# Two chunks' products with the old states interleaved in the first segment, one chunk with its heads in changed rows

## The chip, the cores and the metric

The kernel runs on one core of a Trainium2 chip. The time is that of the device in microseconds (us), from the start of the program on the core to its end; several executions are taken and the median counts. The engines of a core work side by side, each on its own list of instructions in order: PE (TensorE, matrix products), DVE (VectorE), ACT (ScalarE) and POOL (GpSimd). SP (SyncE) only issues loads and stores (DMA) here. An instruction that waits holds up everything behind it on its own engine, and nothing else.

## What is computed

A recurrent attention (RetNet) and behind it a gated feed-forward block, in 32-bit floats:

```python
# q, k, v: (B, H, S, D) = (4, 8, 768, 64)
gamma = 1.0 - 2.0 ** (-5.0 - np.arange(H))
state = zeros(B, H, D, D)
for t in range(S):
    state = gamma[None, :, None, None] * state + einsum('bhd,bhe->bhde', k[:, :, t], v[:, :, t])
    y[:, :, t] = einsum('bhd,bhde->bhe', q[:, :, t], state) / sqrt(D)
x = y.transpose(0, 2, 1, 3).reshape(3072, 512)
g, val = x @ w_gate, x @ w_val          # 512 x 1536 each
out = (g / (1 + exp(-g)) * val) @ w_out  # 1536 x 512
```

The weights arrive as 64-bit floats, and the kernel converts them itself.

## The kernel before

**Tiling.** The sequence of each batch is cut into 6 chunks of 128 positions, and a segment is three chunks of two batches. Four segments make the work. Within a chunk, attention is done with matrix products: scores of q and k under a mask of decays, times v, plus q (scaled by the decay since the chunk's start) times the old state that the chunks before left behind; then the state is decayed and grown by k and v. The feed-forward part of the segment follows: the up part with 12 slices of 128 columns of w_gate and w_val (units f = 0 to 11), the down part with 12 row blocks of w_out. Operands of those products are split into three terms of a shorter format (the tiles `oitem`, `gitem`, `xa`: near_a, near_b, near_c for weights, far_a, far_b, far_c for x), on ACT, DVE and POOL.

**The first segment** (its chunks are numbered n = 0 to 5: n even is the first batch, n odd the second) has to do everything at once: load q, k and v, do the attention, load the weights' 64-bit words, convert them, store the converted ones for the later segments, and run the products. A written plan, `PLAN`, sets the order in which all instructions are issued, and so the order on each engine. Its letters (table at line 577) are:

- `l n:w` loads chunk n's k (w = 0), q (1), v (2), k by rows (3); `U`, `V` load words of weights (unit 0's w_gate with `U0`, its w_val with `V0`; `U12` is the first of w_out); `A` loads tables; `Z` stores a converted unit.
- `s` scores (PE) and masks (DVE); `r`, `t` (state) and `g` (decay of the state, ACT); `m` scores times v (PE) and far_a; `x` far_b and far_c; `o` the product of q with the old state (PE, `mix_old`, line 726); `q`/`Q` scale q with the table qdec on POOL/DVE; `k`/`K`/`E` scale k on POOL/DVE/ACT.
- `a`, `b`, `c` on ACT and `S`, `C` on DVE are the steps that convert a piece of a weight; `T` makes the differences of a unit's parts that later segments need (`sums_t`, line 563), on DVE; `n` the near split of unit f; `p`, `v`, `u`, `y` its products for one chunk, the gate and their product, which empties the PSUM bank (line 948).

**The product with the old state** has 64 rows (the head's dimension) in, 64 out and 128 positions. Two heads lie one above the other: the upper half of the partitions holds head 2n, the lower half head 2n + 1, for q, k and the state. `mix_old` takes the eight heads in turn, so that two of the four quadrants of the PE array are used in turn, upper rows to upper columns and lower rows to lower columns:

```python
for k, (n, i, to) in enumerate(y_parts(c)[1]):
    r = ds(D * i, D)
    nc.tensor.matmul(to, prev[r, n], qd[r, n], start=k < 2, ...)
```

**Loads.** All loads go through SP's queue in the plan's order and use eight completion semaphores in turn, so that an issue waits for the load eight before it. `w_load` (line 1128) brings the blocks of w_out in the down part: in the last segment in two pieces for f < 3, else in one.

Of the kernel before, what the change touches and what calls it, by code (L numbers as in the profile page):

```python
# [25 lines left out]
L = 3  # L26
TH = L * P
NSEG = B * NCK // (2 * L)
# [21 lines left out]

PLAN = """
    A0 I0 l0:0 l1:0 A2 A1 U0:0 s0 a0:1 r1 l0:2 s1 b0:1 A4 A3 l2:1 l2:0 r0 m0 K0 S0:1 c0:1 l1:2 x0:1
    t0 s2 E1 l3:0 l3:1 m1 l2:3 C0:1 g2 V0:0 a0:0 Q2 n0:0 b0:0 l2:2 x1:2 s3 x1:1 n0:1 l4:1 l4:0 l3:2
    t1 S0:0 k2 x0:2 q3 c0:0 C0:0 o2 U1:1 m2 o3 n0:3 s4 m3 a1:1 n0:4 x2:1 l5:1 l3:3 b1:1 x2:2 x3:1
    S1:1 t2 n0:2 p0:0 q4 a1:0 x3:2 c1:1 n0:5 k3 C1:1 g3 b1:0 n1:0 v0:0 l5:0 U2:3 s5 S1:0 t3 c1:0
    C1:0 l5:2 p0:1 n1:1 u0:0 u0:1 T0:0 q5 v0:1 a2 l4:2 b2 y0:1 o5 y0:0 o4 n1:3 S2 n1:2 m5 T0:1 n1:4
    c2 m4 n1:5 x5:2 p1:0 l5:3 x5:1 p1:1 u1:0 C2 v1:0 U3:1 T0:2 x4:2 T1:0 U12:0 a3 v1:1 y1:0 x4:1
    T1:1 L b3 p0:2 a12 c12 n2:0 S3 u1:1 T1:2 b12 u0:2 U4:3 c3 Z0 n2:1 v0:2 Z1 n2:3 S12 y1:1 a4 n2:2
    p1:2 v1:2 C3 u1:2 n2:4 G2:0 y0:2 C12 G2:1 n3:0 U13:1 y1:2 n3:1 n2:5 b4 T2:0 n3:2 S4 U5:2 n3:3
    c13 T2:1 W2:0 Z12 W2:1 h0 c4 i2:1 n3:4 i2:0 G3:0 n3:5 T3:0 C4 T2:2 T3:1 U6:3 j2:0 a5 G3:1 T3:2  # L60
    j2:1 Z2 n4:0 U7:0 W3:0 i3:0 n4:1 b5 n4:2 n4:3 S5 n4:4 W3:1 i3:1 n4:5 c5 G4:0 C5 n5:0 a6 b6 a13
    l4:3 T4:0 j3:0 G4:1 n5:1 j3:1 Z3 T4:1 n5:3 i4:0 n5:2 T4:2 S6 W4:0 b13 c6 i4:1 n5:4 a7 S13 C6
# [246 lines left out]
T0, UP0 = 30.0, 8.35  # L309
# [61 lines left out]
def tile_retnet_swiglu(  # L371
# [13 lines left out]
    nc = tc.nc  # L385
# [30 lines left out]
    loads = place("loads", 3 * UNIT + 256)  # L416
# [6 lines left out]
    warm = place("warm", P + 32)  # L423
# [36 lines left out]
    chunks = {}  # L460

    def load_chunk(n, w, queue=nc.sync):
        c = cs[n]
        t = early[4 * n + w]
        chunks.setdefault(c, {})[w] = t
        queue.dma_start(out=t, in_=(k_t, q_t, v_n, k_n)[w][c])  # L466

    def seg_chunks(s):
        p, pos = divmod(s * L, NCK)
# [5 lines left out]
    T3, B22, B12, T1, B21, B11, T2, T4 = 0, 1, 2, 2, 3, 4, 5, 6  # L475
# [87 lines left out]
    def sums_t(piece, parts=range(3)):  # L563
        kind, a = piece
        w = wt[a]
        flat = w.rearrange("p a b -> p (a b)")
        n = KH * P
        pair = flat[:, : 4 * n].rearrange("p (a b) -> p a b", b=2 * n)[:, :, :n]
        for o, x, y in [((pair, w[:, ds(B22, 2)], w[:, B12 : B11 + 1 : 2])),
                          ((w[:, T2], w[:, B22], w[:, T1])),  # L570
                          ((w[:, T4], w[:, B21], w[:, T2]))][parts[0] : parts[-1] + 1]:
            both(o, x, y, sub)


    pieces = [("up", f) for f in range(NF)] + [("down", a) for a in range(NF // 2)]

    parts = {
        "s": lambda n: scores(cs[n]), "o": lambda n: mix_old(cs[n]),
        "m": lambda n: mix(cs[n]), "x": lambda n, p: split_x(cs[n], p[0]),
        "g": lambda n: decay(cs[n]), "t": lambda n: state(cs[n]),  # L580
        "E": lambda n: scale_k_act(cs[n]),
        "r": lambda n: rows_of(n), "I": lambda n: unit_of(), "B": lambda n: small_tables(),
        "R": lambda n: decay_rows(), "D": lambda n: spread_rows(), "F": lambda n: keep_rows(),
        "k": lambda n: scale_k(cs[n]), "q": lambda n: scale_q(cs[n]),
# [36 lines left out]
    def pairs(t):  # L621
        return t.rearrange("p (n t) -> p n t", n=NP)

    def state_of(c, old=0):
        return states[:, (c + old) % 2, c // NCK % 2]

    def scores(c):
        kt, qt = (pairs(chunks[c][w]) for w in range(2))
        sp = [bank("y" if cs.index(c) == 1 else "s") for i in range(2)]
        for n in range(NP):  # L630
            for i in range(2):
                r = ds(D * i, D)
                nc.tensor.matmul(sp[i][:, ts(n, P)], kt[r, n], qt[r, n],  # L633
                                 start=(n == 0), stop=True, skip_group_check=True)
        a = []
        for i in range(2):
            j = turn["a"] = turn.get("a", -1) + 1
            t = pairs(tmp[:, ts(j % 4, 512)] if j < 10 else loads[:, ts(j - 2, 512)])
            nc.vector.tensor_tensor(t, pairs(sp[i]), mask[:, i], op=ALU.mult)
            a.append(t)  # L640
        att[c] = a


    def scale_q(c, engine=nc.gpsimd):
        if c % NCK:
            qt = pairs(chunks[c][1])
            chunks[c][1] = loads[:, ts(cs.index(c) + 2, 512)]
            engine.tensor_tensor(pairs(chunks[c][1]), qt, qdec, op=ALU.mult)

    def scale_k(c, engine=nc.gpsimd):  # L650
        if c % NCK < NCK - 1:
# [14 lines left out]
    def unit_of():  # L666
        nc.vector.tensor_scalar(unit, mask[:, 0, 0], 0.124, None, op0=ALU.is_ge)
# [21 lines left out]
    def rows_of(n):  # L689
# [4 lines left out]
            nc.tensor.transpose(t[:, ts(m, P)], kt[:, m], unit)  # L694
        chunks[c][3], turned[c] = early[4 * n + 3], t

    def decay(c):

        if 0 < c % NCK < NCK - 1:
            for n in range(NP):  # L700
                nc.scalar.activation(state_of(c)[:, n], state_of(c, 1)[:, n], AF.Copy,
                                     scale=gdec[:, ds(n, 1)])

    def state(c):
        ci = c % NCK
        if ci == NCK - 1:
            return
        vn, kd = chunks[c][2], chunks[c][3]
        new = state_of(c)
        st = banks[6][:, : NP * D]  # L710
        st = st.rearrange("p (n e) -> p n e", n=NP)
        for n in range(NP):
            for i in range(2):
                h = ts(2 * n + i, D)
                nc.tensor.matmul(st[ds(D * i, D), n], kd[:, h], vn[:, h],  # L715
                                 start=(n == 0), stop=True, skip_group_check=True)
        if ci == 0:
            nc.scalar.copy(new, st)
        else:
            nc.vector.tensor_tensor(new, new, st, op=ALU.add)  # L720

    def y_parts(c):
        y = pairs(banks[(0, 1, 2, 3, 7, 6)[first_chunks.index(c)]])
        return y, [(n, i, y[ds(D * i, D), n]) for n in range(NP) for i in range(2)]

    def mix_old(c):
        qd, prev = pairs(chunks[c][1]), state_of(c, 1)
        for k, (n, i, to) in enumerate(y_parts(c)[1]):
            r = ds(D * i, D)
            nc.tensor.matmul(to, prev[r, n], qd[r, n], start=k < 2, stop=False,  # L730
                             skip_group_check=True)

    def x_of(c):
        i, j = c // NCK % 2, c % L
# [2 lines left out]
    def split_x(c, part):  # L737
        (far_b, far_c)[part - 1](x_of(c), y_parts(c)[0])
# [15 lines left out]
    lmask = local[:, : 2 * NP * HC].rearrange("p (i n) -> p i n", i=2)  # L754
    lk, lg = local[:, ds(2 * NP * HC, H)], local[:, ds(2 * NP * HC + H, NP)]
    spare = tab[:, : 2 * 512]
    half = [ds(0, D), ds(D, D)]
    given = {}
    R0 = 6

# [367 lines left out]
    def w_load(s, t, f, first):  # L1128
        def load():
            wo[f] = item("o", DM)  # L1130
            o = wo[f].bitcast(U32)
            if first:
                nc.sync.dma_start(out=o[:, 2], in_=w_dn[f].bitcast(U32))
            else:
                for i in (slice(2), slice(2, 3)) if s == NSEG - 1 and f < 3 else (slice(None),):
                    nc.sync.dma_start(out=o[:, i], in_=w_dn3[f][:, i])

        def o():
            return [wo[f][:, i] for i in range(3)]
# [117 lines left out]
    cs = seg_chunks(0)  # L1257
# [21 lines left out]
    t = down_stage(0, end)  # L1279
    for s in range(1, NSEG):  # L1280
# [8 lines left out]
        t = down_stage(s, t)  # L1289
# [50 lines left out]
```

## Time and profile before

| what | value |
|---|---|
| median of three runs | 642.5 us (642.07 to 642.75) |
| profiled execution | 642.54 us |
| its span, first to last instruction | 640.5 us |
| granted PE clock | 1.00 throughout |
| busy: PE, DVE, ACT, POOL | 632.9, 484.1, 394.3, 261.1 us |
| loads and stores | 139.6 MB, 218 GB/s on average |
| PE matmuls of the old states' product (line 730) | 64 passes, 269 ns each, 16.3 to 32.3 us |
| DVE's scaling of q (line 648) | 1, 1269 ns |
| POOL's scaling of q (line 648) | 3, 1271 to 1728 ns |
| DVE's differences of unit 0 | 0.69, 0.42 and 0.42 us, at 30.8, 33.4 and 36.6 |

A 32-bit product appears as two passes of PE in the trace, so 8 products are 16 passes. Passes overlap in the array: the 269 ns are one pass from end to end, while 16 of them start within 1.02 us. A busy share says how long an engine worked; whether it holds up the others is read from who waited for whom. The span has about 18 us at its start in which the first data arrive, and 622 us behind it.

### The profile page before, as it was taken

How to read it: one execution, taken by the hardware profiler on the slowest of the kernel's cores; microseconds unless marked ns; L12 is line 12 of the kernel's file. 1: busy time of each engine (PE TensorE's matmuls, PEld its weight loads, DVE VectorE, ACT ScalarE, POOL GpSimd, SP SyncE). 2: the span in 40 equal slices, each digit the busy share in tenths (PEclk: the TensorE clock that was granted, in tenths of full speed). 3: DMA queues.
4: the chain of work that ended last, by engine and by line, in shares of the span. 5: the costliest groups of instructions: out<-in, count | busy, mean ns of one | idle time of the engine just before them, and what ended most of it. 6: DMA issues, size and time to landing. Idle time of an engine off the chain costs nothing.

```text
span 640.5 us, 14132 instructions
## 1 busy us (share of the span) xinstructions
PE 632.9 (99%) x5587; PEld 580.4 (91%) x5587; DVE 484.1 (76%) x715; ACT 394.3 (62%) x868; POOL 261.1 (41%) x172
## 2 busy tenths in 40 slices
PE   7999999999999999999999999999999999999997
PEld 6899999987779999997778999998777999999886
DVE  4998787899898887665797869575789866768361
ACT  4787797777865565566766555564785555654221
POOL 1534445544425866630003665550101666663000
PEclk9999999999999999999999999999999999999999
DMA  9899998798787445258765640457776444304564
GB/s 320 291 332 326 376 329 269 268 326 305 266 285 278 168 148 173 75 179 260 247 239 214 211 152 15 175 196 246 226 258 248 154 164 173 116 1 151 194 214 148
DMA packets 50626, 139.60 MB, mean 218 GB/s; under 512 B 5120, under 2 KB 18176, under 8 KB 50560
## 3 DMA queue, kind: packets, MB, share of 16 engines
q1 hardware_dynamic: 49984, 137.92, 62.6%
q8 instruction: 44, 0.72, 0.5%
q10 hardware_dynamic: 576, 0.79, 0.3%
q14 instruction: 22, 0.18, 0.1%
HBM read 108.80 MB, written 29.88 MB: 217 GB/s over the span
## 4 chain that ended last, share of the span: by engine, by line
PE 97%; DMA 3%; SPq 0%; DVE 0%; ACT 0%; issue 0%
PE bank L1088 41%; PE bank L1157 32%; PE bank L919 13%; PE bank L789 6%; PE bank L937 3%; DMA hT<-in_v_n_dram 2%; PE bank L744 1%; DMA hT<-in_q_t_dram 1%; PE bank L730 0%; PE bank L715 0%; PE bank L633 0%; DVE chunk_x L1178 0%; SPq L513 0%; ACT chunk_x L1180 0%; SPq L466 0%
## 5 line engine op out<-in xcount | busy, mean ns | idle before, releaser
L1157 PE MATMUL bank<-oitem,gitem 128*128 128x512 f32 x867 | 208.2, 394 | 0.0
L1157 PEld LDWEIGHTS bank<-oitem,gitem 128*128 128x128 f32 x867 | 159.6, 188 | 34.5 <-DVE tmp L812 0.4
L997 POOL TENSOR_TENSOR gitem<-gitem 128x768 fp32r<-128x768 f32 x71 | 138.7, 1963 | 117.9 <-DVE gitem L994 99.0
L1088 PE MATMUL bank<-xa,gitem 128*128 128x384 f32 x864 | 160.5, 334 | 0.0
L1088 PEld LDWEIGHTS bank<-xa,gitem 128*128 128x128 f32 x864 | 150.8, 188 | 0.2
L997 POOL TENSOR_TENSOR oitem<-oitem 128x256 fp32r<-128x256 f32 (+1 forms) x60 | 64.1, 1074 | 56.8 <-DVE oitem L994 48.3
L1088 PE MATMUL bank<-xb,gitem 128*128 128x384 f32 x432 | 84.5, 334 | 0.0
L919 PE MATMUL bank<-xa,oitem 128*128 128x384 f32 x480 | 84.3, 335 | 0.0
L919 PEld LDWEIGHTS bank<-xa,oitem 128*128 128x128 f32 x480 | 83.0, 188 | 0.4 <-ACT tmp L444 0.2
L994 DVE SCALAR_TENSOR_TENSOR gitem<-gitem,loads 128x768 fp32r<-128x768 f32 x72 | 75.1, 1057 | 9.1 <-ACT gitem L991 7.5
L1088 PEld LDWEIGHTS bank<-xb,gitem 128*128 128x128 f32 x432 | 75.9, 188 | 0.4
L991 ACT ACTIVATE gitem<-loads 128x768 fp32r<-128x768 f32 x72 | 59.6, 843 | 26.0 <-PE bank L1088 16.8
L994 DVE SCALAR_TENSOR_TENSOR gitem<-gitem,hT 128x768 fp32r<-128x768 f32 x48 | 46.1, 965 | 24.4 <-ACT gitem L991 24.4
L991 ACT ACTIVATE gitem<-hT 128x768 fp32r<-128x768 f32 x48 | 40.2, 842 | 31.4 <-PE bank L1157 29.4
L1022 ACT COPY chunk_x<-bank 64x128 f32<-64x128 f32 x144 | 36.6, 260 | 32.6 <-PE bank L789 21.3
L401 DVE SCALAR_TENSOR_TENSOR gitem<-gitem 128x768 fp32r<-128x768 f32 x49 | 49.7, 1022 | 1.3 <-DVE gitem L994 0.5
L816 POOL TENSOR_TENSOR loads<-loads,tab 128x512 f32<-128x512 f32 x9 | 13.4, 1493 | 82.1 <-PE bank L789 44.6
L1088 PE MATMUL bank<-xb,oitem 128*128 128x384 f32 x216 | 43.4, 335 | 0.0
L1088 PEld LDWEIGHTS bank<-xb,oitem 128*128 128x128 f32 x216 | 37.9, 188 | 0.3
L994 DVE SCALAR_TENSOR_TENSOR oitem<-oitem,loads 128x256 fp32r<-128x256 f32 (+1 forms) x42 | 34.5, 824 | 2.1 <-ACT oitem L991 2.1
L1105 DVE TENSOR_TENSOR hT<-bank,tmp 128x384 f32<-128x384 f32 x36 | 20.0, 555 | 20.7 <-PE bank L1088 20.4
L1103 ACT COPY tmp<-bank 128x384 f32<-128x384 f32 x36 | 17.2, 478 | 28.3 <-PE bank L1088 19.3
(118 smaller groups left out, 789.8 us busy)
## 6 DMA issues: line engine op xcount, KB each, us to landing
loads<-wup SPq DMA_DIRECT2D x36, 896.0 KB, 4.7
oitem<-wdnt SPq DMA_DIRECT2D x33, 768.0 KB, 4.4
wdnt<-oitem SPq DMA_DIRECT2D x12, 768.0 KB, 5.5
wup<-first SPq DMA_DIRECT2D x9, 896.0 KB, 6.7
rawp<-in_w_gate_dram SPq DMA_DIRECT2D x12, 512.0 KB, 6.8
rawp<-in_w_val_dram SPq DMA_DIRECT2D x12, 512.0 KB, 6.2
rawp<-in_w_out_dram SPq DMA_DIRECT2D x12, 512.0 KB, 5.7
out_dram<-chunk_x SPq DMA_DIRECT2D x21, 256.0 KB, 2.1
```

What stands on the lines that cost most here:

```text
L401: stt(o, x, 1.0, y, op0=mul, op1=op)
L789: nc.tensor.matmul(o, a, b, start=start, stop=True, skip_group_check=True)
L919: nc.tensor.matmul(o, w[:, a, ts(b, P)], X0[:, a, i, NC - 1 - b], start=a == b == 0, stop=a == 2 and b == NC - 1, skip_group_check=True)
L937: nc.tensor.matmul(o, w[:, a, ts(b, P)], X0[:, a, :, NC - 1 - b, ts(j, P)], start=a == b == 0, stop=a == 2 and b == NC - 1, skip_group_che ...
L991: act(o[0], x, AF.Copy, scale=CUT / FAR)
L994: stt(o[1], f32(o[0]), -FAR, x, op0=mul, op1=add)
L997: op(o[2], f32(o[0]), f32(o[1]), op=add)
L1022: copy(cx[half[i], ds(2 * h, 2), c, half[z]], y.rearrange("p (b t) -> p b t", b=2))
L1088: nc.tensor.matmul(o, w[:, a, k], x[:, a, KH - 1 - k], start=start and a == k == 0, stop=a == 2 and k == KH - 1, skip_group_check=True)
L1103: steps = (lambda: copy(p1, x), lambda: tt(c11, z, p1, op=add), lambda: act(gate, c11, AF.Silu, scale=ONE), lambda: copy(u2, x), lambda: c ...
L1105: lambda: copy(p5, wb), lambda: tt(h1, x, p5, op=add),
L1157: nc.tensor.matmul(banks[tok][:, cols], hs[f][:, a, ds(i * TH + u * P, P)], wo[f][:, a, cols], start=f == a == 0, stop=f == NF - 1 and a = ...
```

## The change

`mix_old` now takes two chunks, n and n + 1, and issues their products in turn, head by head. For the second of the two, the heads lie with the halves exchanged ("turned over"): the lower half holds head 2n, the upper one head 2n + 1. Its products go from lower rows to upper columns and from upper rows to lower columns, so that four products in a row lie in four different quadrants. The two chunks write different PSUM banks. To have it so, for the second batch's chunks 3 and 5:

- their k and q are loaded in two halves each, with the halves exchanged (four loads become eight); the scores come out exchanged too and are swapped back by name;
- the state that chunk 1 and chunk 3 leave is written with its halves exchanged (an index of the product), and the decays take a turned copy of their table: two small copies on ACT. Chunk 5's decay turns the state back: eight instructions of 64 partitions where four of 128 were;
- q is scaled with a turned copy of qdec: two copies of 64x512 on DVE.

The product of chunk 3 moves ahead of m2, together with chunk 2's; in the plan q2 becomes POOL's (it was DVE's `Q2`) and stands ahead of q3 and k2. On ACT, the copy of chunk 1's state moves ahead of `a0:0`, `n0:0` and `b0:0`. `sums_t` of unit 0 runs on POOL instead of DVE. In the last segment, `w_load` brings w_out in two pieces for f < 7.

```diff
--- before.py
+++ after.py
@@ -50,16 +50,16 @@
-    t0 s2 E1 l3:0 l3:1 m1 l2:3 C0:1 g2 V0:0 a0:0 Q2 n0:0 b0:0 l2:2 x1:2 s3 x1:1 n0:1 l4:1 l4:0 l3:2
-    t1 S0:0 k2 x0:2 q3 c0:0 C0:0 o2 U1:1 m2 o3 n0:3 s4 m3 a1:1 n0:4 x2:1 l5:1 l3:3 b1:1 x2:2 x3:1
-    S1:1 t2 n0:2 p0:0 q4 a1:0 x3:2 c1:1 n0:5 k3 C1:1 g3 b1:0 n1:0 v0:0 l5:0 U2:3 s5 S1:0 t3 c1:0
-    C1:0 l5:2 p0:1 n1:1 u0:0 u0:1 T0:0 q5 v0:1 a2 l4:2 b2 y0:1 o5 y0:0 o4 n1:3 S2 n1:2 m5 T0:1 n1:4
...
+    e0 e1 t0 s2 q2 E1 l3:0 l3:1 m1 e2 l2:3 C0:1 g2 V0:0 l2:2 x1:2 s3 q3 t1 a0:0 n0:0 b0:0 x1:1 n0:1
+    l4:1 l4:0 l3:2 S0:0 k2 x0:2 c0:0 C0:0 U1:1 o2 m2 s4 n0:3 m3 a1:1 n0:4 x2:1 l5:1 l3:3 b1:1 x2:2
+    x3:1 S1:1 t2 n0:2 p0:0 q4 a1:0 x3:2 c1:1 n0:5 k3 C1:1 g3 b1:0 n1:0 v0:0 l5:0 U2:3 s5 S1:0 t3
+    c1:0 C1:0 l5:2 p0:1 n1:1 u0:0 u0:1 q5 T0:0 v0:1 a2 l4:2 b2 y0:1 y0:0 o4 n1:3 S2 n1:2 m5 T0:1
+    n1:4 c2 m4 n1:5 x5:2 p1:0 l5:3 x5:1 p1:1 u1:0 C2 v1:0 U3:1 T0:2 x4:2 T1:0 U12:0 a3 v1:1 y1:0
...
@@ -463,7 +463,17 @@
         c = cs[n]
         t = early[4 * n + w]
         chunks.setdefault(c, {})[w] = t
-        queue.dma_start(out=t, in_=(k_t, q_t, v_n, k_n)[w][c])
+        src = (k_t, q_t, v_n, k_n)[w][c]
+        if w < 2 and turned_over(c):
+            for m in range(2):
+                queue.dma_start(out=t[half[m]], in_=src[half[1 - m]])
+            return
+        queue.dma_start(out=t, in_=src)
+
+    half = [ds(0, D), ds(D, D)]
+
+    def turned_over(c):
+        return c // NCK % 2 == 1 and c % NCK > 0
 
     def seg_chunks(s):
         p, pos = divmod(s * L, NCK)
@@ -569,16 +579,16 @@
         for o, x, y in [((pair, w[:, ds(B22, 2)], w[:, B12 : B11 + 1 : 2])),
                           ((w[:, T2], w[:, B22], w[:, T1])),
                           ((w[:, T4], w[:, B21], w[:, T2]))][parts[0] : parts[-1] + 1]:
-            both(o, x, y, sub)
+            (pool if a < 1 else both)(o, x, y, op=sub)
 
 
     pieces = [("up", f) for f in range(NF)] + [("down", a) for a in range(NF // 2)]
 
     parts = {
-        "s": lambda n: scores(cs[n]), "o": lambda n: mix_old(cs[n]),
+        "s": lambda n: scores(cs[n]), "o": lambda n: mix_old(cs[n], cs[n + 1]),
         "m": lambda n: mix(cs[n]), "x": lambda n, p: split_x(cs[n], p[0]),
         "g": lambda n: decay(cs[n]), "t": lambda n: state(cs[n]),
-        "E": lambda n: scale_k_act(cs[n]),
+        "E": lambda n: scale_k_act(cs[n]), "e": lambda n: turn_tables(n),
         "r": lambda n: rows_of(n), "I": lambda n: unit_of(), "B": lambda n: small_tables(),
         "R": lambda n: decay_rows(), "D": lambda n: spread_rows(), "F": lambda n: keep_rows(),
         "k": lambda n: scale_k(cs[n]), "q": lambda n: scale_q(cs[n]),
@@ -629,10 +639,12 @@
         sp = [bank("y" if cs.index(c) == 1 else "s") for i in range(2)]
         for n in range(NP):
             for i in range(2):
-                r = ds(D * i, D)
+                r = half[i]
                 nc.tensor.matmul(sp[i][:, ts(n, P)], kt[r, n], qt[r, n],
                                  start=(n == 0), stop=True, skip_group_check=True)
         a = []
+        if turned_over(c):
+            sp = sp[::-1]
         for i in range(2):
             j = turn["a"] = turn.get("a", -1) + 1
             t = pairs(tmp[:, ts(j % 4, 512)] if j < 10 else loads[:, ts(j - 2, 512)])
@@ -645,7 +657,18 @@
         if c % NCK:
             qt = pairs(chunks[c][1])
             chunks[c][1] = loads[:, ts(cs.index(c) + 2, 512)]
-            engine.tensor_tensor(pairs(chunks[c][1]), qt, qdec, op=ALU.mult)
+            engine.tensor_tensor(pairs(chunks[c][1]), qt, qturn if turned_over(c) else qdec,
+                                 op=ALU.mult)
+
+    qturn = pairs(loads[:, :512])
+    gturn = warm[:, ds(P + 8, NP)]
+
+    def turn_tables(m):
+        if m < 2:
+            nc.vector.tensor_scalar(qturn[half[m]], qdec[half[1 - m]], 1.0, None, op0=mul)
+            return
+        for m in range(2):
+            act(gturn[half[m]], gdec[half[1 - m]], AF.Copy)
 
     def scale_k(c, engine=nc.gpsimd):
         if c % NCK < NCK - 1:
@@ -694,12 +717,22 @@
             nc.tensor.transpose(t[:, ts(m, P)], kt[:, m], unit)
         chunks[c][3], turned[c] = early[4 * n + 3], t
 
+    def other(c):
+        return c // NCK % 2 == 1 and c % NCK < L - 1
+
     def decay(c):
 
         if 0 < c % NCK < NCK - 1:
+            new, was = state_of(c), state_of(c, 1)
             for n in range(NP):
-                nc.scalar.activation(state_of(c)[:, n], state_of(c, 1)[:, n], AF.Copy,
-                                     scale=gdec[:, ds(n, 1)])
+                if not turned_over(c):
+                    act(new[:, n], was[:, n], AF.Copy, scale=gdec[:, ds(n, 1)])
+                elif other(c):
+                    act(new[:, n], was[:, n], AF.Copy, scale=gturn[:, ds(n, 1)])
+                else:
+                    for m in range(2):
+                        act(new[half[m], n], was[half[1 - m], n], AF.Copy,
+                            scale=gturn[half[1 - m], ds(n, 1)])
 
     def state(c):
         ci = c % NCK
@@ -712,7 +745,7 @@
         for n in range(NP):
             for i in range(2):
                 h = ts(2 * n + i, D)
-                nc.tensor.matmul(st[ds(D * i, D), n], kd[:, h], vn[:, h],
+                nc.tensor.matmul(st[half[i ^ other(c)], n], kd[:, h], vn[:, h],
                                  start=(n == 0), stop=True, skip_group_check=True)
         if ci == 0:
             nc.scalar.copy(new, st)
@@ -723,12 +756,13 @@
         y = pairs(banks[(0, 1, 2, 3, 7, 6)[first_chunks.index(c)]])
         return y, [(n, i, y[ds(D * i, D), n]) for n in range(NP) for i in range(2)]
 
-    def mix_old(c):
-        qd, prev = pairs(chunks[c][1]), state_of(c, 1)
-        for k, (n, i, to) in enumerate(y_parts(c)[1]):
-            r = ds(D * i, D)
-            nc.tensor.matmul(to, prev[r, n], qd[r, n], start=k < 2, stop=False,
-                             skip_group_check=True)
+    def mix_old(c, d):
+        parts = [(pairs(chunks[e][1]), state_of(e, 1), y_parts(e)[1]) for e in (c, d)]
+        for k in range(2 * NP):
+            for x, (qd, prev, to) in enumerate(parts):
+                n, i, o = to[k]
+                nc.tensor.matmul(o, prev[half[i ^ x], n], qd[half[i ^ x], n], start=k < 2,
+                                 stop=False, skip_group_check=True)
 
     def x_of(c):
         i, j = c // NCK % 2, c % L
@@ -754,7 +788,6 @@
     lmask = local[:, : 2 * NP * HC].rearrange("p (i n) -> p i n", i=2)
     lk, lg = local[:, ds(2 * NP * HC, H)], local[:, ds(2 * NP * HC + H, NP)]
     spare = tab[:, : 2 * 512]
-    half = [ds(0, D), ds(D, D)]
     given = {}
     R0 = 6
 
@@ -1132,7 +1165,7 @@
             if first:
                 nc.sync.dma_start(out=o[:, 2], in_=w_dn[f].bitcast(U32))
             else:
-                for i in (slice(2), slice(2, 3)) if s == NSEG - 1 and f < 3 else (slice(None),):
+                for i in (slice(2), slice(2, 3)) if s == NSEG - 1 and f < 7 else (slice(None),):
                     nc.sync.dma_start(out=o[:, i], in_=w_dn3[f][:, i])
 
         def o():
```

More of the change, by code (lines that the diff above doesn't have):

```diff
@@ L52 @@
     A0 I0 l0:0 l1:0 A2 A1 U0:0 s0 a0:1 r1 l0:2 s1 b0:1 A4 A3 l2:1 l2:0 r0 m0 K0 S0:1 c0:1 l1:2 x0:1
-    t0 s2 E1 l3:0 l3:1 m1 l2:3 C0:1 g2 V0:0 a0:0 Q2 n0:0 b0:0 l2:2 x1:2 s3 x1:1 n0:1 l4:1 l4:0 l3:2
-    t1 S0:0 k2 x0:2 q3 c0:0 C0:0 o2 U1:1 m2 o3 n0:3 s4 m3 a1:1 n0:4 x2:1 l5:1 l3:3 b1:1 x2:2 x3:1
-    S1:1 t2 n0:2 p0:0 q4 a1:0 x3:2 c1:1 n0:5 k3 C1:1 g3 b1:0 n1:0 v0:0 l5:0 U2:3 s5 S1:0 t3 c1:0
-    C1:0 l5:2 p0:1 n1:1 u0:0 u0:1 T0:0 q5 v0:1 a2 l4:2 b2 y0:1 o5 y0:0 o4 n1:3 S2 n1:2 m5 T0:1 n1:4
[L57 to L62, printed above, removed]
+    e0 e1 t0 s2 q2 E1 l3:0 l3:1 m1 e2 l2:3 C0:1 g2 V0:0 l2:2 x1:2 s3 q3 t1 a0:0 n0:0 b0:0 x1:1 n0:1
[3 more added lines that the diff above has]
+    n1:4 c2 m4 n1:5 x5:2 p1:0 l5:3 x5:1 p1:1 u1:0 C2 v1:0 U3:1 T0:2 x4:2 T1:0 U12:0 a3 v1:1 y1:0
+    x4:1 T1:1 L b3 p0:2 a12 c12 n2:0 S3 u1:1 T1:2 b12 u0:2 U4:3 c3 Z0 n2:1 v0:2 Z1 n2:3 S12 y1:1 a4
+    n2:2 p1:2 v1:2 C3 u1:2 n2:4 G2:0 y0:2 C12 G2:1 n3:0 U13:1 y1:2 n3:1 n2:5 b4 T2:0 n3:2 S4 U5:2
+    n3:3 c13 T2:1 W2:0 Z12 W2:1 h0 c4 i2:1 n3:4 i2:0 G3:0 n3:5 T3:0 C4 T2:2 T3:1 U6:3 j2:0 a5 G3:1
+    T3:2 j2:1 Z2 n4:0 U7:0 W3:0 i3:0 n4:1 b5 n4:2 n4:3 S5 n4:4 W3:1 i3:1 n4:5 c5 G4:0 C5 n5:0 a6 b6
+    a13 l4:3 T4:0 j3:0 G4:1 n5:1 j3:1 Z3 T4:1 n5:3 i4:0 n5:2 T4:2 S6 W4:0 b13 c6 i4:1 n5:4 a7 S13 C6
     W4:1 n6:0 T5:0 U8:2 Z4 b7 U14:3 n5:5 n6:1 G5:0 j4:1 S7 C13 j4:0 G5:1 n6:2 a8 n6:3 P2 n6:4 i5:1
```

## The prediction

> **What bounds the kernel now.** First the list of who waited for whom on PE: engine and line, the releaser, total us, times, longest.
>
> ```profile
> PE bank L633 <- DMA hT<-in_k_t_dram: 1.4, 2, 0.9
> PE bank L744 <- DMA hT<-in_v_n_dram: 1.2, 2, 0.6
> PE bank L1253 <- DVE warm L1268: 1.1, 1, 1.1
> PE bank L633 <- DVE tmp L639: 0.4, 1, 0.4
> ```
>
> That is all PE waited for in 640.5 us, and the table by stages shows where: 4.1 us of idle before 18 us, none from 18 to 196.
>
> ```profile
> 0.00:18.00 18.00, 13.91 (x170) 11.98 (x170) 9.94 (x17) 9.31 (x24) 2.93 (x6) 1.00 0.94 327
> 18.00:32.00 14.00, 14.00 (x188) 13.01 (x190) 13.41 (x24) 10.07 (x20) 7.04 (x6) 1.00 0.85 278
> ```
>
> (Stretch, its length, busy us of PE, weight loads, DVE, ACT, GpSimd, clock, DMA share, GB/s.) So time is won by less PE work after 18 us or by filling a wait before it, as long as nothing that feeds PE becomes late. The PE timeline (start, us, ... what ended the idle time) has the work concerned:
>
> ```profile
> 15.56 0.69 PE L715 MATMUL bank<-hT 128*64 128x64 f32 x16
> 16.25 1.09 PE L730 MATMUL bank<-loads,states 64*64 64x128 f32 x16
> 17.97 1.09 PE L744 MATMUL bank<-tmp,hT 128*64 128x128 f32 x16 [0.63 <-DMA hT<-in_v_n_dram]
> 18.99 1.09 PE L730 MATMUL bank<-loads,states 64*64 64x128 f32 x16
> 20.02 1.16 PE L633 MATMUL bank<-hT 64*128 64x128 f32 x16
> 30.43 1.96 PE L730 MATMUL bank<-loads,states 64*64 64x128 f32 x32
> ```
>
> L730 is the old states' product: chunk 2 (16.25) and chunk 3 (18.99) with m2 between them, waiting for its v until 17.97; chunks 4 and 5 together at 30.43. Last, the timelines of DVE, ACT and SP give the chain that could make PE wait:
>
> ```profile
> 14.93 1.27 DVE L648 TENSOR_TENSOR loads<-hT,tab 128x512 f32<-128x512 f32 x1
> 19.12 0.68 DVE L547 SCALAR_TENSOR_TENSOR bank<-first,bank 128x512 uint32<-128x512 uint32 x1
> 16.62 0.62 ACT L991 ACTIVATE oitem<-first 128x512 fp32r<-128x512 f32 x1
> 17.66 0.36 ACT L718 COPY states<-bank 128x256 f32<-128x256 f32 x1
> 28.86 0.69 ACT L540 ACTIVATE first<-rawp 128x512 int32<-128x512 uint32 x1 [0.64 <-DVE bank L547]
> 29.57 0.38 SPq L513 DMA_DIRECT2D rawp<-in_w_val_dram  x1
> 39.24 1.16 ACT L534 ACTIVATE first<-rawp 128x1024 f32<-128x1024 f32 x1 [0.36 <-DMA rawp<-in_w_out_dram]
> 43.97 0.42 DVE L948 TENSOR_TENSOR hT<-bank,tmp 128x256 f32<-128x256 f32 x1
> ```
>
> Read backwards: L948 empties bank 3 at 44.39. Its next user is the eighth group of twelve L937 matmuls of 0.12 us that began at 34.22: 34.22 + 7 x 12 x 0.12 = 44.3. Slack: none. L948 stands on DVE behind two L547 that wait for ACT's conversion of w_out, whose data arrived at 39.24; that load left SP after the one at 29.57, and SP got its buffer when L540 ended (28.86 + 0.69 = 29.55). L540 waited for DVE, which shows no idle time over 0.2 us from 13.12 to 28.8. So PE at 44.4 hangs on DVE's queue at 13 to 20 us.
>
> **The pairs on PE.** Removed: two lone streams of 16 passes (1.02 us each from start to start, 2.04) and one of 32 (30.43 to 32.32, 1.89). Added: two streams of 32 passes over four quadrants of 64x64 where two were used. The nearest row is L789, which fills four quadrants with 64 columns: 64 passes in 1.09 us, 17 ns each, against 64 ns for L730's 128 columns. Twice the columns: 34 ns, so 32 passes take 1.09. Saved: 0.95 and 0.80, 1.75 at most. Bounds: nothing (64 ns a pass as now), and 17 ns a pass if a pass is all that counts (3.93 - 2 x 0.54 = 2.85). I take 1.09, the row with all four quadrants.
>
> **Where the first pair starts.** It stands ahead of m2, so it must wait for what only chunk 3 waited for: t1, then ACT's copy of the state. Before t1, DVE makes the turned q table with two copies of 64x512. Its gap of 0.87 (12.26 to 13.12) holds them in part: from 0.23 each (128 elements at 4.40, L667) to 0.68 (512 elements, L401), and 1.27 against GpSimd (L648). I take 0.68, spaced 0.60: masks start at 13.36 for 13.12, and s3 and t1 on PE slide 0.24. t1 ends at 16.49, ACT copies to 16.91, the pair runs from 16.97 to about 18.0, and m2 starts at 18.05 for 17.97: its v landed at 17.93, so the pair lies in the old wait. Chunk 3's 1.02 us is gone behind m2; s4 needs its k load (19.1, when its slot served SP again), so PE is some 0.8 us ahead at 20, and 1.5 to 1.6 at 33.
>
> **Who is late next.** DVE loses Q2 (L648, 1.19 from start to start) and pays 0.24: 0.95 ahead. But the plan moves the state copy ahead of a0:0 on ACT: that conversion, started at 16.04, now waits for t1 and starts at 16.80, and L991 behind it ends at 18.00 for 17.24. DVE's L994, until now at 18.51, waits for it: 18.05. Then L547 18.65 for 19.12, L540 28.36 for 28.86, SP's load, w_out and L948 all about 0.5 earlier: bank 3 is free at 43.9. PE arrives at 42.9 and gives 1.0 back. What stays is **0.5 us**.
>
> The table copies run while GpSimd makes q2 (its q lands at 11.1; L648 there 1.27, so until 12.5). Row: DVE's L648 took 1.27 beside a GpSimd product, a like size from PSUM 0.68, and GpSimd's own L648 1.73 for 1.27. [...]
>
> **The rest.** GpSimd takes q2 (1.27) ahead of q3 and k2; k2 then ends near 16.3 and is first used at 22. Its three T0 products replace DVE's 0.69, 0.42 and 0.42; by GpSimd's rows (1.27 for 512 elements, 1.07 mean of L997 on oitem) 1.3, 1.1, 1.1, laid in its idle stretches of 4.28 (from 26.7) and 7.13 (from 35.8). Uncovered they would hold back the near_c products behind them by about 1 us. ACT gets two tiny copies (0.1 to 0.2, inside its wait for t1) and at g5 four more state products (0.24 apart, 1.0), while ACT is busy 64 of 80 us there: nothing. Four early loads come in halves: four more SP issues of 0.33 to 0.51, and four more of the load slots (rival three). The last segment's W loads come in two pieces for four more f: PE has no wait for a load there, and SP is idle: nothing; uncovered, 0.4 each.
>
> **Sum.** 640.5 - 0.5 = 640.0 of span. The profiled run took 642.54, so 2.04 lies around its span, and it is the median of the three (642.5): forecast 642.0.
>
> **Rivals.** *One: the quadrants don't overlap.* L730's two quadrants give 64 ns a pass, no better than a full-height L744 (68), so nobody has shown 128 columns in four. The pair then takes 2.04 (16.97 to 19.01), m2 ends at 20.03, where s4 stood before: PE gains nothing, 642.5. Against it: L789 runs four. [...] L789 keeps each bank to one row tile, and the pair doesn't. But L730 puts both row tiles into one bank already, in different partitions, and no row prices that. Chance 0.13.
>
> *Two: PE keeps it all.* If a0:0's delay costs nothing behind it and DVE's 0.95 ahead, with T0's 1.5 off it, carries to 44.4, bank 3 is not late and PE keeps 1.6: 640.9. For it: DVE is what the chain queued on. Against: ACT at 39.24 waits for a load, which DVE's later freedom doesn't bring sooner. Chance 0.21.
>
> *Three, slower: the half loads cost slots.* SP's waits show that from 4.58 each issue waits for an earlier load to land, eight in flight. Halves take whole slots, so what follows goes later: V0's w_val from 10.06 to 11.2, k5's second half from 17.94 to 19.2. If each lands as long after its issue as now, k5 (6.9) is whole at 26.1 and s5, at 25.66, waits; with the 8.9 us of q5, at 28.1. In the middle, 27.1, s5 is 1.45 late, and so are its masks on DVE and L547, L540 and L948 behind them: 643.9. It decides from a landing at 25.7. Against it: SP's issues at 11.12, 11.81, 12.48, 13.15, 13.84 are 0.68 apart because loads land at that pace, one full queue, and the bytes in it stay the same. Chance 0.20.
>
> **How the numbers follow.** The forecast has 0.46: 641.4 to 642.4 by the copies' bounds (0.23 each: masks not late, 0.7 kept; 1.27: only one of the two can meet q2, about 0.1 kept). A measurement can't tell less than 0.2% (1.3 us) from no change. Faster than 641.2 is rival two: 0.21. Slower than 643.8 is most of rival three: 0.18. Within are the forecast, rival one and the rest: 0.61. The range, 640.9 to 643.9, leaves about 0.1 outside at each end.
>
> **What would show it.** L764 (the old L730) at about 34 ns a pass, the pair at 17.0 and ended by 18.1; m2's wait nearly gone; PE ahead by 0.8 at 21 and 1.5 at 36; a new PE wait of about 0.7 to 1 before 44, for DVE's mul or ACT; ACT's L534 at 16.8; DVE's copies 0.4 to 0.7 each. It is wrong if the passes stay at 64 ns, if s5 waits for a load, or if no wait appears near 44.

## The result, and the profile after

The changed kernel takes 646.0 us (median of six runs, 645.54 to 646.93) where the kernel before took 642.6 beside it (six runs): ratio 1.0055, 95% interval 1.0042 to 1.0068. It is slower by half a per cent. A second set of runs, taken later among the experiments, gave 1.0032 (1.0020 to 1.0044). The profiled execution has a span of 644.4 us, against 640.5.

Who waited for whom on PE, changed kernel (same view as before):

```profile
PE bank L643 <- DMA hT<-in_k_t_dram: 1.9, 2, 1.2
PE bank L643 <- DMA first<-in_k_t_dram: 1.6, 1, 1.6
...
PE bank L778 <- DMA hT<-in_v_n_dram: 0.5, 1, 0.5
PE bank L764 <- ACT states L751: 0.2, 1, 0.2
```

The wait for v ahead of the scores times v is down from 1.2 to 0.5: what is left is the first chunk's, and the third chunk's (0.63 in the kernel before, at 17.97) is gone, as meant. New is 1.6 us for keys that land in `first`: these are the sixth chunk's, one of the two chunks whose loads were cut into upper and lower half. The table by stages (PE, weight loads, DVE, ACT, GpSimd, granted clock, DMA share, GB/s) shows where:

```profile
0.00:18.00 18.00, 13.49 (x154) 11.57 (x154) 9.36 (x17) 8.09 (x23) 3.39 (x7) 1.00 0.94 292
18.00:32.00 14.00, 11.93 (x155) 10.69 (x154) 11.14 (x19) 8.71 (x18) 7.69 (x7) 0.88 1.02 301
28.00:32.00 4.00, 3.98 (x35) 3.59 (x36) 2.61 (x5) 2.10 (x7) 2.89 (x3) 0.57 0.85 294
```

Before 18 us the DMA share is 0.94 as before, but the rate is 292 GB/s for 327: the transfers keep the DMA engines as busy and bring less. From 18 to 32 us PE is idle for 2.1 us, where it was never idle. In this execution the granted clock fell to half as well, from 28.6 to 32.0. PE's timeline:

```profile
17.07 0.69 PE L748 MATMUL bank<-hT 128*64 128x64 f32 x16
17.68 0.43 PE L764 MATMUL bank<-loads,states 64*64 64x128 f32 x2
18.34 1.10 PE L764 MATMUL bank<-loads,states 64*64 64x128 f32 x30 [0.23 <-ACT states L751]
19.37 1.09 PE L778 MATMUL bank<-tmp,hT 128*64 128x128 f32 x16
...
28.02 2.24 PE L643 MATMUL bank<-first 64*128 64x128 f32 x16 [1.62 <-DMA first<-in_k_t_dram]
```

The pair (L764) and the scores times v behind it (L778) are where the change puts them. Then the sixth chunk's scores start at 28.02 instead of 25.66, 2.36 late, and run at half rate (2.24 us for 1.16). The chain of waits that leads there (start, us, what) is made of loads alone:

```profile
7.37 6.13 DMA hT<-in_v_n_dram
13.50 0.02 issue
13.52 6.36 DMA hT<-in_q_t_dram
19.87 0.02 issue
19.89 8.00 DMA first<-in_k_t_dram
27.88 0.14 issue
28.02 2.24 PE bank L643 x16
```

Each load is issued as soon as the load eight before it has landed (13.50, 19.87), and the last one is the sixth chunk's keys. The positions on PE, after minus before: 1.03 us at the fourth chunk's scores (15.50 for 14.47), 2.36 at the sixth's, 3.88 at the start of the unit's products behind them and 4.18 at their end, 3.33 once the second pair has given 0.85 back, 3.1 to 3.8 from 100 to 600 us, 3.9 at the end.

How fast the half loads went can be read from the landings. For three 256 KB loads' worth in a row (the fourth chunk's keys and queries and one load behind them; the sixth chunk's queries and keys and one load between them), from the first landing part of the load ahead to that of the last:

```
kernel                         fourth chunk   sixth chunk
before                              2.05          2.05 us
changed, first profile              3.44          3.35
changed, second profile             2.91          2.98
```

Two of the three are cut in half in the changed kernel. The second profile is that of run 8 below. Taking 0.68 for the whole one (2.05 / 3), a half load of 128 KB holds the queue for 0.56 us ((2.91 - 0.68) / 4) to 0.69 ((3.44 - 0.68) / 4), about as long as a whole one of 256 KB.

### The profile page after: what moved, and what is told of

Its sections match the earlier page's. It is cut to its first block, busy times and chain, and to the rows that moved or that the text cites. A ratio compares the mean times of both kernels' runs of the same rounds, so it can differ in the third digit from the quotient of the medians.

```text
span 644.4 us, 14162 instructions
## 1 busy us (share of the span) xinstructions
PE 634.0 (98%) x5587; PEld 581.0 (90%) x5587; DVE 483.5 (75%) x713; ACT 396.2 (61%) x874; POOL 263.5 (41%) x176
## 4 chain that ended last, share of the span: by engine, by line
PE 95%; DMA 4%; SPq 0%; issue 0%; DVE 0%; ACTq 0%; ACT 0%
PE bank L1121 41%; PE bank L1190 32%; PE bank L952 13%; PE bank L822 6%; PE bank L970 2%; DMA hT<-in_q_t_dram 2%; DMA first<-in_k_t_dram 1%; DMA hT<-in_v_n_dram 1%; PE bank L748 0%; PE bank L643 0%; PE bank L778 0%; PE bank L764 0%; SPq L471 0%; DVE chunk_x L1211 0%; ACTq L471 0%
## 5 line engine op out<-in xcount | busy, mean ns | idle before, releaser
L1024 ACT ACTIVATE gitem<-loads 128x768 fp32r<-128x768 f32 x72 | 59.6, 843 | 26.1 <-PE bank L1121 16.8
L1136 ACT COPY tmp<-bank 128x384 f32<-128x384 f32 x36 | 17.2, 478 | 28.6 <-PE bank L1121 19.6
```

The costliest lines, as they stand in the source:

```text
L1024: act(o[0], x, AF.Copy, scale=CUT / FAR)
L1136: steps = (lambda: copy(p1, x), lambda: tt(c11, z, p1, op=add), lambda: act(gate, c11, AF.Silu, scale=ONE), lambda: copy(u2, x), lambda: c ...
```

## The experiments

Ratios are to the kernel before, run beside each, with 95% intervals.

**1. The loads whole again.** The change as it is, but the two chunks' upper and lower halves are exchanged in the layout of the inputs, on the host, so that one load of 128 rows suffices:

```diff
-        if w < 2 and turned_over(c):
-            for m in range(2):
-                queue.dma_start(out=t[half[m]], in_=src[half[1 - m]])
-            return
...
+    for n in ("q_t", "k_t"):
+        t = given[n]
+        t[NCK + 1 : NCK + 3] = np.concatenate(
+            [t[NCK + 1 : NCK + 3, D:], t[NCK + 1 : NCK + 3, :D]], axis=1)
```

> The changed kernel, but k and q of chunks 3 and 5 come in four whole loads of 128 rows instead of eight of 64; their halves are exchanged beforehand in the layout of the input. Theory (a load of 64 rows holds the load queue nearly as long as one of 128, and everything behind it is late by some 0.55 us for each of four): the loads arrive as before the change, k of chunk 5 at about 25 us instead of 28.2, PE has no wait of 1.6 us before s5 and no half clock, and the time is 641.5 to 642.5. Rival (the order of the plan, the copy of the state ahead of the conversion on ACT, or the work moved to GpSimd makes it late): still 644.5 or more.

Measured: 643.07 us, ratio 0.9999 (0.9987 to 1.0010). The loss is gone, so it came with the half loads; three loads' worth take 2.03 us at both places. But no gain is left either. The profiled execution shows one reason, at its very start:

```profile
6.08 2.08 PE L639 MATMUL bank<-hT 64*128 64x128 f32 x16 [1.22 <-DMA hT<-in_k_t_dram]
8.09 1.11 PE L713 MATMUL bank<-loads,hT 128*128 128x128 f32 x4
9.13 1.62 PE L639 MATMUL bank<-hT 64*128 64x128 f32 x16
```

The first scores take 2.08 us where the profiles of before and after have 1.16. PE ran at half rate until about 10.1 us, and all that follows from these scores, VectorE's chain above all, began 1.2 us late.

**2 and 3. Half loads without the change.** The kernel before, with the same four loads in two pieces each: once upper and lower half of the rows, once left and right half of each row.

```diff
-        queue.dma_start(out=t, in_=(k_t, q_t, v_n, k_n)[w][c])
+        src = (k_t, q_t, v_n, k_n)[w][c]
+        if w < 2 and n in (3, 5):
+            for m in range(2):
+                queue.dma_start(out=t[ds(D * m, D)], in_=src[ds(D * m, D)])
+            return
+        queue.dma_start(out=t, in_=src)
```

(Left and right: `t[:, ts(m, 256)]` and `src[:, ts(m, 256)]`.)

> The kernel before, with k and q of chunks 3 and 5 each in two loads of 64 rows, and nothing else changed. Theory: k of chunk 5 whole at 27 us or later instead of 24.9, PE idle for over 1 us before s5, and 645 to 646.5. Rival (it is the plan, not the loads): 642.3 to 643.

> The kernel before, with the same four arrays each in two loads of 128 rows and 256 columns: as many loads and slots as with half rows, the same bytes. Theory that half the rows are what is slow: each piece holds the queue for about 0.34 us, and 642.5 to 643.3. Rival (each further load takes one of eight slots and is issued later, whatever its shape): as with half rows, 645 or more.

Measured: halves of the rows 645.87 us, 1.0046 (1.0031 to 1.0061); halves of the columns 643.23 us, 1.0005 (0.9991 to 1.0018). The number of loads, their issues and the slots that they take are the same in both. So none of these makes the loss; the pieces of 64 rows do. The granted clock stayed at 1.00 in the run with half rows, so the loss needs no fall of the clock either. The stages from 18 to 24 us, first with half rows, then with half columns:

```profile
18.00:24.00 6.00, 4.92 (x82) 4.39 (x83) 4.27 (x8) 3.47 (x7) 2.55 (x3) 1.00 1.09 322
```

```profile
18.00:24.00 6.00, 6.00 (x93) 5.47 (x90) 5.83 (x10) 3.59 (x6) 3.48 (x3) 1.00 1.09 355
```

With the same DMA share (1.09) the half rows bring 322 GB/s for 355, and PE is idle for 1.1 of these 6 us. Three loads' worth took 3.02 and 3.31 us with half rows, 2.19 and 2.18 with half columns.

**4. Which rows.** The same again, with every second row in each piece:

```diff
-                queue.dma_start(out=t[ds(D * m, D)], in_=src[ds(D * m, D)])
+                queue.dma_start(out=t[m::2], in_=src[m::2])
```

> The kernel before with the same four loads in two pieces of 64 rows again, but each piece takes every second row (even ones, then odd ones) instead of the upper or the lower half. In the run with upper and lower halves the next load's first part landed 0.4 to 0.5 us after a half's, where a whole load of twice the bytes takes 0.68, and the ratio was 1.0046; with all 128 rows and half of each row's length it took 0.37 to 0.40 and the ratio was 1.0005. Theory A, where the rows lie decides (64 neighbouring partitions can't be written as fast as 128, but 64 that are spread over all of them can): pieces land 0.34 to 0.42 us apart, three loads' worth in 2.1 to 2.3 us, ratio 0.9990 to 1.0012. Theory B, the number of rows in a load decides, wherever they lie: three loads' worth in 2.9 to 3.3 us, TensorE waits for the sixth chunk's keys, ratio 1.0035 to 1.0060.

Measured: 651.32 us, 1.0124 (1.0108 to 1.0141). Neither theory has this ratio, but SP's queue explains it:

```profile
21.14 1.20 SPq L469 DMA_DIRECT2D first<-in_q_t_dram  x2
...
27.18 1.11 SPq L469 DMA_DIRECT2D first<-in_k_t_dram  x2
```

The loads into `first` are issued at 21.14 and 27.18, when DVE has just finished a write into that same tile (instructions at 20.42 and 26.48, 0.69 and 0.68 us long). In the kernel before they left at 14.55 and 17.94. With strided rows they got a wait that they didn't have, so the time answers another question. The fourth chunk's pieces go into `hT` and have no such wait, and there the pace can be read: their first parts landed at 12.23, 12.56, 12.91 and 13.25, and three loads' worth took 2.05 us, as with whole loads. So theory A holds for the pace (2.1 to 2.3 expected): 64 rows spread over all partitions are as fast as 128 (2.05 us both), 64 neighbouring ones are not (2.91 to 3.44 in the changed kernel, 3.02 and 3.31 in the one before). Its ratio is not shown. And pieces of other partitions also read other rows of the memory that they come from; no run separates the two sides.

**5. PE kept busy during the wait, first try.** Six warm-up products ahead of the sixth chunk's scores in the plan:

```diff
-    ... l5:0 U2:3 s5 S1:0 t3
+    ... l5:0 U2:3 w w w w w w s5 S1:0 t3
```

> The changed kernel with six more products of the warm-up tile on PE ahead of s5 (work without a use, in a bank that is free then), in the time in which PE waits for k of chunk 5. Theory that the half clock from 28.6 to 32.0 us follows from this idle time and costs half of 3.4 us: the clock stays whole and the time is 644.0 to 644.8. Rival (the passes of s5 and t3 are slow for another reason): 645.7 to 646.3, with s5 still at about 2.2 us.

Measured: 647.48 us, 1.0078 (1.0053 to 1.0103), slower than the changed kernel. The experiment was ill-built, as its PE timeline says:

```profile
28.49 2.62 PE L1286 MATMUL bank<-warm 128*128 128x128 f32 x12 [2.24 <-DVE xa L1040]
31.04 1.73 PE L643 MATMUL bank<-first 64*128 64x128 f32 x16
```

The warm-up products write bank 3 and stood 2.24 us behind its reader on DVE. They filled no wait but made one, and the scores came 3 us later still. The clock fell here too, to half from 28.86 to 32.27, so the theory wasn't tested.

**6. PE kept busy, second try,** in the bank that the scores write anyway:

```diff
+        if c == cs[5]:
+            for _ in range(6):
+                nc.tensor.matmul(sp[0][:, :P], warm[:, :P], warm[:, :P], start=True, stop=True,
+                                 skip_group_check=True)
```

> The changed kernel (half loads) with six warm-up products just ahead of the scores of the sixth chunk, in the bank that these scores write anyway, so that they wait for no reader; in the earlier run with warm-up products they wrote to another bank and stood 2.24 us behind its reader. Theory: TensorE is busy while it waits for the two halves of the sixth chunk's keys, the granted clock stays at 1.0 from 28 to 32 us, the scores still start at 27.9 to 28.2, and 1.2 to 1.7 us are saved: ratio to the kernel before 1.002 to 1.0037 (644.0 to 645.1). Rival: the work behind it is bound by loads and conversions, so the clock costs nothing: 1.005 to 1.006.

Measured: 644.71 us, 1.0033 (1.0019 to 1.0047). The clock stayed at 1.00 and the scores started at 28.17, with 0.24 of idle time left. That is within the forecast, but the changed kernel itself came out at 1.0032 in its second set of runs (run 8). So what the fall of the clock at 28 us costs isn't shown. How seldom it comes is on record: of 24 executions of the changed kernel, with eight or eleven warm-up products at the start, two have a mean granted clock under 0.999 (0.996 at 646.28 us, 0.997 at 646.05). The profile shown in the first section is one of these two.

**7. A longer warm-up at the start.** Eleven products in place of eight, in the kernel before, in the changed one, and in the one with whole loads:

```diff
-    warm_up(8)
+    warm_up(11)
```

> The kernel before with eleven warm-up products at the start in place of eight (same numbers, written to a bank that nobody reads yet). In the profiled execution with whole loads TensorE stood idle 1.22 us ahead of the first scores and then ran them at half clock (16 passes in 2.08 us), in the kernel before it was idle 0.92 us and ran them at full clock (1.16 us). Theory: the longer warm-up ends near 5.5 us and leaves less than 0.6 us idle, so no execution starts at half clock; where the kernel before hardly ever falls into it, this changes nothing: ratio 0.999 to 1.0005. Rival: most executions of the kernel before start at half clock and the profiled one is an exception: ratio 0.998 or lower.

> The changed kernel (half loads) with eleven warm-up products in place of eight. Theory: its start was at full clock already (16 passes in 1.16 us after 1.15 us idle), and the late loads set the rest: ratio to the kernel before 1.004 to 1.0055. Rival: a late start is a good part of its loss: ratio 1.002 or lower.

> The changed kernel with whole 128-row loads and eleven warm-up products in place of eight. Theory: the gain of the pair was hidden in the run with whole loads by the half clock from 6.1 to 9.5 us, which set the whole VectorE chain of the first 30 us back by some 1.2 us; with the start at full clock the ratio to the kernel before is 0.9975 to 0.999 (641.2 to 642.1), and TensorE doesn't wait for VectorE in the big run of products at 45 us. Rival: the gain is given back to the conversions on ScalarE and VectorE whatever the start is: ratio 0.9995 to 1.0005, with a wait of TensorE between 40 and 50 us.

Measured: before 642.35 us, 0.9992 (0.9983 to 1.0001), its highest run 643.02 where the kernel before has 644.75; changed 644.20, 1.0019 (1.0007 to 1.0030); whole loads **641.78, 0.9981 (0.9972 to 0.9991)**, the fastest of all. With the start out of the way, the half loads cost 2.4 us (644.20 against 641.78). The rest of the change gains 0.57 by the medians (642.35 against 641.78), which is at the edge of what these runs can tell: the intervals of the two ratios overlap. The changed kernel came out as its rival has it, but without the longer warm-up it has 1.0032 in run 8, and those two intervals overlap as well. The chain that ended last on the way to bank 3, whole loads and longer warm-up:

```profile
16.27 0.37 ACT states L747
16.64 0.58 ACT first L540
17.22 0.53 ACT oitem L1020
17.75 0.02 issue
17.77 0.69 DVE oitem L1023
18.46 0.62 DVE bank L553
...
33.37 1.30 POOL oitem L1026
34.66 0.72 POOL first L578
35.38 0.02 issue
35.40 6.62 DMA wup<-first
42.01 0.00 issue
42.01 0.68 DVE first L553
42.69 0.35 DVE hT L977
43.04 0.04 issue
43.09 1.70 PE bank L966 x12
```

It begins and ends as the prediction has it: the state's copy ahead of a conversion on ACT, DVE behind them, and at 43 us the product that empties bank 3 (L977, the L948 of before) with PE waiting for it, 0.16 us. The ratio is the theory's, but that short wait is one that the theory ruled out. Between them the chain names not the load of w_out, as predicted, but GpSimd's last T0 product (L578) and the store behind it. That store seems to have cost nothing: DVE was in the L553 just ahead, begun at 41.41, and starts such products 0.60 apart, so it would have come to this one at 42.01 anyway.

**8. The changed kernel once more.**

> The changed kernel itself once more, so that it can be compared with its variants on one chip and with more runs. With eleven warm-up products it came out at 1.0019 times the kernel before, and in its first runs without them at 1.0055. Theory: its loss is two things, late half loads (some 0.3%) and a TensorE that comes late to full clock in many executions (some 0.3%, gone with the longer warm-up): ratio 1.0040 to 1.0065. Rival: the first runs were on a chip that served the half loads more slowly: ratio here 1.001 to 1.003, as with the longer warm-up.

Measured: 644.74 us, 1.0032 (1.0020 to 1.0044), between the two theories. This time the half loads were faster (the table in the first section), the sixth chunk's scores started at 26.87 after 1.1 us of waiting, and the clock stayed at 1.00.

**9. The pair's passes one chunk after the other,** on the kernel with whole loads and longer warm-up:

```diff
-        for k in range(2 * NP):
-            for x, (qd, prev, to) in enumerate(parts):
+        for x, (qd, prev, to) in enumerate(parts):
+            for k in range(2 * NP):
```

> The changed kernel with whole loads and eleven warm-up products, and the two chunks' products with the old states issued one chunk after the other instead of pass by pass in turn; everything else stays. Theory: the overlap of the two halves of the rows is what saves TensorE time (32 passes in 1.10 us interleaved, 1.96 us in the kernel before with one chunk after the other), for each of the two pairs; of these 1.7 us some 0.6 to 1.2 us last to the end: ratio 0.9990 to 1.0005 (the interleaved one has 0.9981). Rival: what it gained comes from the rest of the change and the overlap is hidden behind the conversions: ratio 0.9975 to 0.9985.

Measured: 641.90 us, 0.9986 (0.9976 to 0.9997). The interleaved one has 0.9981; the intervals overlap, so no gain from the interleaving is shown at the end. PE's timeline, interleaved and then one after the other:

```profile
16.12 0.43 PE L760 MATMUL bank<-loads,states 64*64 64x128 f32 x2
16.78 1.10 PE L760 MATMUL bank<-loads,states 64*64 64x128 f32 x30 [0.23 <-ACT states L747]
17.83 1.09 PE L774 MATMUL bank<-tmp,hT 128*64 128x128 f32 x16
...
29.65 1.10 PE L760 MATMUL bank<-loads,states 64*64 64x128 f32 x32
```

```profile
16.11 1.75 PE L760 MATMUL bank<-loads,states 64*64 64x128 f32 x32
17.89 1.09 PE L774 MATMUL bank<-tmp,hT 128*64 128x128 f32 x16
...
29.88 1.59 PE L760 MATMUL bank<-loads,states 64*64 64x128 f32 x32
```

The first pair gains nothing: interleaved, its second chunk's first pass waits for ACT's copy of the state with everything behind it, and both versions are done by 17.9. The second pair gains 0.49.

**10. The q product back on DVE,** same base: `s2 Q2 E1` for `s2 q2 E1` in the plan.

> The changed kernel with whole loads and eleven warm-up products, and the second chunk's q product on VectorE again (0.69 us there, 1.27 us on GpSimd). Theory: VectorE's chain of the first 30 us sets when the conversions end, so 0.5 to 0.7 us more on it come out at the end: ratio 0.9988 to 0.9996. Rival: that chain has slack there: 0.9976 to 0.9986, as with the product on GpSimd.

Measured: 642.36 us, 0.9992 (0.9983 to 1.0000). That is 0.6 us slower than with the product on GpSimd (641.78) by the medians, but the intervals overlap, so the worth at the end isn't shown. The trace shows the way: on DVE the product took 1.40 us and not 0.69 (from 14.18, while GpSimd made its own from 13.76), DVE came to its conversion product (L1023) at 18.49 instead of 17.77, bank 3 was free at 43.92 instead of 43.04, and PE waited 0.39 us for it instead of 0.16.

## Why the prediction was wrong, by its own steps

**The step that failed** is in rival three. The sum has nothing for the four loads cut in half; their price was left to that rival (chance 0.20), and it was dismissed because loads land 0.68 apart, "one full queue, and the bytes in it stay the same". The bytes stayed the same and the pace didn't: a load of 64 neighbouring rows holds the queue for 0.56 to 0.69 us, not for half of 0.68. Four loads cut in half put 1.8 to 2.7 us more into a queue (the table's two rows, less 2 x 2.05) that was full from the start to 25 us, and the sixth chunk's scores had only 0.8 us of slack to it (keys whole at 24.88, scores at 25.66 in the kernel before). The kernel before with nothing but these halves lost 0.46% (3.1 us by the medians), and with the pieces cut the other way nothing that can be told. Slots, which the rival named as the mechanism, weren't it.

**The rival's size** was off as well. Of its two landings, 26.1 and 28.1 for the sixth chunk's keys, it took the middle; 28.25 was measured in the first profile and 27.13 in the second. And it stopped at the wait. In the first profile the clock fell to half behind it, which took the delay from 2.36 us at the scores to 4.18 behind the unit's products. The 1.3 us between the first and the second set of runs isn't that fall, though: the five other executions of the first set had a granted clock of 0.999 or more and took 645.54 to 646.93. How much of it is the pace of the half loads (2.9 to 3.4 us for three loads' worth), and how much the rate of the first passes, half or full, stays open. Nor is the wait ahead of the sixth chunk's scores always the whole loss: in the second profile PE is 0.8 us behind the kernel before at 60 us and 2.1 near the end, and 0.7 of this comes by 81 us, where PE waits 0.41 us for ACT.

**The pairs on PE: right in size, not in worth.** 32 passes in 1.10 us, 34 ns each; 1.09 was forecast. Rival one, quadrants that don't overlap, is out. Each bank took passes of both row tiles (upper and lower half of the rows) in turn, which no row had priced: they came at these 34 ns. But the saving of 0.95 and 0.80 was reckoned against the order of before (2.04 and 1.89 from start to start). With one chunk after the other in the new order the two pairs take 1.75 and 1.59, so against that order the interleaving gave nothing at the first pair and 0.49 at the second.

**Where the first pair starts: right once the loads are whole.** Scores of the fourth chunk at 14.42 (14.71 forecast), the pair's first passes at 16.12 and the rest, behind ACT's copy, at 16.78 (16.97), scores times v at 17.83 (18.05). The pair lies in the old wait and needn't be fast. In the changed kernel it came at 17.68, with the loads 1 us late.

**The table copies on DVE** took 0.97, 0.93 and 0.86 us for the two; 2 x 0.68 was forecast, between bounds of 0.23 and 1.27 each. The upper bound was a product on DVE beside one on GpSimd. With whole loads and the longer warm-up the first copy began at 12.11, while GpSimd's product ran from 11.05 to 12.33, so it didn't wait for that one's end. It took 0.50 us, and 0.42 in the runs where no product ran beside it (runs 1 and 10). Where these 0.08 us come from isn't shown. The bound's price, masks late, didn't come: they started at 13.07, 13.36 was forecast.

**Who is late next: right in the path, wrong in the size of the wait.** With whole loads and the longer warm-up the conversion behind the state's copy started at 16.54 (16.80 forecast), the next one on ACT ended at 17.74 (18.00), DVE took over at 17.77 (18.05), bank 3 was free at 43.0 (43.9), and PE waited for it, but 0.16 us where 1.0 was forecast. The load of w_out between them, which the forecast's path goes over, is in the chain of run 10 (issued at 30.98, landed at 38.70). PE was 1.36 us ahead of the kernel before with the same warm-up after the second pair (30.69 for 32.05; 1.5 to 1.6 was forecast) and 0.95 at 45 us (44.62 for 45.57); the wait is 0.16 of these 0.41, and the rest isn't accounted for. What stayed was 0.57 by the medians, where 0.5 was forecast. That the two agree is in part luck: in the two profiled executions the lead at the end is 1.4 us (638.8 for 640.2; the first is the fastest of its twelve). Rival two, PE keeps it all, is not shown in the medians.

**GpSimd's three T0 products** took 1.27, 0.75 and 0.74 us (1.3, 1.1 and 1.1 forecast), in idle stretches, and no wait for GpSimd appeared on PE. The last segment's W loads in two pieces weren't tried by themselves; from 506 us to the end the difference to the kernel before goes from 3.6 to 3.9 us.

## What to carry to other kernels

Before you cut a load into pieces, look at which partitions each piece covers, not at its bytes: pieces of all partitions with shorter rows cost nothing here that could be told (ratio 1.0005), pieces of 64 neighbouring partitions cost nearly a whole load each (0.56 to 0.69 us against 0.68), and in a full queue that comes out at the first consumer with less slack than the delay (here 0.8 us against 1.8 to 2.7). If rows have to be exchanged, do it where the data is laid out. And ask of a faster step what it waits for: of two pairs that were made faster, one lay in a wait anyway, and the bank that PE needed next hung on the engine that fed the conversions.

## What the hardware showed that was not expected

**When PE comes to full rate.** Warm-up passes take 236 ns at the start (16 in 3.78 us) and 125 ns at 26 us (12 in 1.50, run 6). It varies between programs that are alike up to there: after 0.92, 0.94, 1.05 and 1.15 us of idle time ahead of the first scores they ran at full rate, after 1.14 (run 6) and 1.22 us (run 1) at half until 10.3 and 10.1 us. The granted-clock column shows 1.00 there all the same. The trace's own record of the clock begins only with the first full rate, at 5.26 us in the kernel before and 10.14 in run 1; ahead of that the passes' durations tell. Later a gap of 1.34 us (changed kernel, longer warm-up) left the clock at 1.00. One of 1.62 us was followed by half clock from 28.56 to 31.97, 3.4 us; one of 2.24 (run 5) also by 3.4 us, and one of 5.18 (run 4) by 6.8. Each of these three falls came 23.9 us after the first full rate (4.67 to 28.56, 4.96 to 28.86, 4.51 to 28.40), seven times 3.41. So in these traces the clock changes on a grid of 3.41 us. The gap of 1.34 us left it at full, those of 1.62 and more didn't; what decides between them isn't shown.

**Passes one chunk after the other got faster too:** 32 in 1.59 us in run 9, against 1.96 in the kernel before, though no pass alternates between the chunks. There the second chunk's passes go from upper rows to lower columns and the reverse. The trace shows where the time goes: passes start two per 0.11 us up to 30.37 and from 30.76 on, as in the kernel before, and fourteen start in the 0.39 us between. With the interleaved order the first four passes, one for each quadrant, last 320 ns and all others 269; here two passes of 320 ns start at 30.38, when six of the first chunk's sixteen are still to come. So the second chunk's passes seem to begin beside the first's, and run 9 takes away only a part of the overlap that it was meant to take away.
